# Two first layers, second half of the tokens: block products of a 2x2 scheme in place of the plain matmuls

## The chip, the cores and the metric

One core of one Trainium2 chip runs the whole program. The metric is device time in microseconds (us); lower is better. The engines are TensorE (PE in the profile: matrix products, with PEld for its weight loads), VectorE (DVE), ScalarE (ACT), GpSimd (POOL), and SyncE (SP), which issues most DMAs. Each engine takes its instructions in the order in which the program gives them, and waits on semaphores for the others.

## The reference

```python
def _attn_ref(q, k, v, w_pre, w_post):
    scores = np.matmul(q, k.transpose(0, 1, 3, 2)) / np.sqrt(64)
    scores = np.einsum('bhij,hg->bgij', scores, w_pre)
    scores = scores - np.max(scores, axis=-1, keepdims=True)
    attn = np.exp(scores)
    attn = attn / (np.sum(attn, axis=-1, keepdims=True) + 1e-09)
    attn = np.einsum('bhij,hg->bgij', attn, w_post)
    return np.matmul(attn, v)
def _moe_ref(x, w1, w2, w3, w_out):        # 768 -> 1024 -> 1024 -> 768
    return ((x @ w1) * (x @ w2) @ w3) @ w_out
def _moe2_ref(x, w_in, w_out):             # 768 -> 2048 -> 768
    h = np.maximum(x @ w_in, 0.0)
    return h * h @ w_out
# x = attention output of 4 batches x 448 tokens = 1792 tokens x 768 features
```

The weights of the two mixtures arrive as 64-bit floats and are brought to 32 bits on the chip.

## The kernel before

Attention fills the first 470 us or so. The change leaves it alone. It leaves its output in DRAM as `xd`, four blocks of 448 tokens.

The two mixtures then run over the tokens in two halves of 896, each half as two blocks (t = 0, 1) of 448 columns. Features lie on the partitions. A *unit* is one output chunk of 128 features: `l1` (x times a chunk of w1 or w2), `ly` (the product of both times w3·w_out, which `p34` has multiplied together once), `l3` (w_in, then relu and square) and `l4` (the second w_out). All operands are split into a high part (rounded to the matmul's 32-bit type, `fp32r`) and a low part (the rest), and `mm3` makes three matmuls for each 128-deep chunk: high·high, high·low, low·high. A matmul has 448 columns. An `l1` or `l3` unit has 6 chunks, so 18 matmuls for each block; a `ly` or `l4` unit has 8 chunks, 24 matmuls.

Weights come in pieces of 384 or 512 columns. For each piece, in both halves alike, SP loads the 64-bit words (`raw`), ACT narrows them (L81), DVE joins the bits in three instructions (L93, L95, L97), ACT rounds to the high part (L111) and POOL subtracts for the low part (L115). `Moe.stage` issues these a fixed number of pieces ahead of the unit that PE runs, and `Moe.run` walks the units in order, so the program's order is one list of (unit, block) steps.

## Time and profile before

| | us |
|---|---|
| median of 3 runs | 1355.46 (1354.13 to 1357.52) |
| the profiled execution | 1355.44 |
| its span, first to last instruction | 1353.60 |

Columns of the views: "busy" is the time in which an engine ran instructions, "x" their number, "mean ns" the mean duration of one, "idle before" the time the engine stood still ahead of them and what ended it. Matmuls are pipelined, so their durations overlap. PEclk is the granted TensorE clock, 1.00 being the full 2.4 GHz.

### The profile page before, as it was taken

The numbers are of one execution on the slowest core, as the hardware profiler recorded it, in microseconds if no ns is written. First come the engines' busy times: TensorE is split into PE (matmuls) and PEld (weight loads), VectorE is DVE, ScalarE is ACT, GpSimd is POOL, SyncE is SP. The second block draws the span as 40 slices with busy tenths as digits, with TensorE's granted clock in tenths as the row PEclk, the third lists the DMA queues.
The fourth block names the chain that finished last, engine by engine and source line by source line (L and its number), as shares of the span: only waits on it lengthen the run. The fifth ranks groups of instructions, "written<-read, shape, count | busy, mean of one in ns | idle before, by whom it ended". The sixth has DMA issues, their size and how long they took to land.

```text
span 1353.6 us, 23970 instructions
## 1 busy us (share of the span) xinstructions
PE 1317.1 (97%) x8858; PEld 1144.1 (85%) x8858; DVE 921.8 (68%) x1580; ACT 706.3 (52%) x1525; POOL 385.4 (28%) x405
## 2 busy tenths in 40 slices
PE   6999999999998899999999999999999999999998
PEld 3677777777776788899999999999999999999998
DVE  4898788888787789864228944985555128945972
ACT  5888878878886455433224533543343224533530
POOL 4143153244212312101222322233222222322231
PEclk9999999999999899999999999999999999999999
DMA  6565475466445556664123432465433133433441
GB/s 190 168 190 170 136 213 182 129 186 193 133 129 161 146 157 168 194 172 121 56 82 105 133 113 82 119 200 165 126 115 94 55 86 101 133 118 82 121 152 55
DMA packets 97033, 183.76 MB, mean 136 GB/s; under 512 B 20693, under 2 KB 63701, under 8 KB 96469
## 3 DMA queue, kind: packets, MB, share of 16 engines
q1 hardware_dynamic: 89717, 178.73, 45.5%
q10 hardware_dynamic: 7200, 3.51, 0.9%
q8 instruction: 70, 1.15, 0.4%
q14 instruction: 46, 0.38, 0.1%
HBM read 129.52 MB, written 14.16 MB: 106 GB/s over the span
## 4 chain that ended last, share of the span: by engine, by line
PE 78%; issue 7%; ACT 5%; DVE 4%; POOL 3%; DMA 2%; SPq 0%; ACTq 0%; POOLq 0%; DVEq 0%
PE l L54 47%; PE y L54 9%; PE sp L285 6%; PE p L54 5%; PE tp L341 5%; PE pv L382 4%; PE sc L259 4%; ACT p L299 2%; DMA kraw<-k 1%; POOL wl L115 1%; ACT ph L324 1%; POOL ql L242 1%; ACT s L270 1%; DMA qraw<-q 1%; DVE nm L291 1%
## 5 line engine op out<-in xcount | busy, mean ns | idle before, releaser
L115 POOL TENSOR_TENSOR wl<-f,wh 128x384 fp32r<-128x384 f32 (+1 forms) x176 | 197.8, 1126 | 566.3 <-ACT wh L111 539.5
L93 DVE TENSOR_SCALAR f<-y 128x384 int32<-128x384 int32 (+1 forms) x208 | 148.6, 714 | 91.8 <-POOL wl L115 88.5
L285 PE MATMUL sp<-r,kpre 120*120 120x448 f32 x360 | 159.4, 565 | 6.6 <-ACT p L299 3.0
L111 ACT ACTIVATE wh<-f 128x384 fp32r<-128x384 f32 (+1 forms) x192 | 106.6, 555 | 104.3 <-DVE f L97 96.0
L299 ACT ACTIVATE p<-sp,nm 120x448 f32<-120x448 f32 x180 | 113.7, 640 | 70.2 <-DVE nm L291 69.6
L54 PE MATMUL l<-bhh,wh 128*128 128x448 f32 x384 | 139.4, 363 | 0.0
L54 PE MATMUL l<-bhh,wl 128*128 128x448 f32 x384 | 139.2, 362 | 0.0
L54 PE MATMUL l<-blh,wh 128*128 128x448 f32 x384 | 138.2, 360 | 0.0
L291 DVE TENSOR_REDUCE nm<-sp 120x1 f32<-120x448 f32 x180 | 108.0, 619 | 42.3 <-PE sp L285 36.2
L97 DVE SCALAR_TENSOR_TENSOR f<-raw,f 128x384 int32<-128x384 int32 (+1 forms) x208 | 130.1, 625 | 7.2
L95 DVE SCALAR_TENSOR_TENSOR f<-y,f 128x384 int32<-128x384 int32 (+1 forms) x208 | 129.0, 620 | 7.0
L341 PEld LDWEIGHTS <-ph 120*128 120x128 f16 (+1 forms) x1440 | 107.7, 99 | 28.3 <-issue 27.9
L331 DVE SCALAR_TENSOR_TENSOR pl<-p,sm,ph 120x448 f16<-120x448 f32 x180 | 124.1, 730 | 0.0
L341 PE MATMUL tp<-kwh,ph 120*128 120x120 f16 x720 | 121.2, 218 | 2.8 <-DVE p L356 2.0
L341 PE MATMUL tp<-kwh,pl 120*128 120x120 f16 x720 | 120.3, 217 | 0.3 <-DVE pl L331 0.3
L341 PE MATMUL tp<-kwl,ph 120*128 120x120 f16 x720 | 120.4, 217 | 0.0
L81 ACT ACTIVATE y<-raw 128x384 f32<-128x384 f32 (+1 forms) x208 | 120.0, 577 | 0.2 <-DMA raw<-w3t 0.2
L324 ACT ACTIVATE ph<-p,sm 120x448 f16<-120x448 f32 x180 | 112.0, 683 | 15.3 <-DVE sm L319 15.1
L259 PE MATMUL sc<-kt,qh 128*110 128x448 f32 (+1 forms) x192 | 100.9, 525 | 9.5 <-DVE kt L220 7.3
L314 POOL TENSOR_SCALAR sm<-sm 120x2 f32<-120x2 f32 (+3 forms) x94 | 30.8, 328 | 276.1 <-ACT p L299 264.5
L285 PEld LDWEIGHTS sp<-r,kpre 120*120 120x120 f32 x360 | 59.2, 185 | 48.7 <-issue 21.9
L270 ACT ACTIVATE s<-sc 110x448 f32<-110x448 f32 (+1 forms) x186 | 90.6, 555 | 9.9 <-PE sc L259 8.0
(115 smaller groups left out, 3114.0 us busy)
## 6 DMA issues: line engine op xcount, KB each, us to landing
r<-s SPq DMA_DIRECT2D x172, 210.0 KB
raw<-w SPq DMA_DIRECT2D x64, 384.0 KB
raw<-win SPq DMA_DIRECT2D x64, 384.0 KB
raw<-wo SPq DMA_DIRECT2D x48, 512.0 KB
kraw<-k SPq DMA_DIRECT2D x22, 448.0 KB
raw<-w3t SPq DMA_DIRECT2D x16, 512.0 KB
qraw<-q SPq DMA_DIRECT2D x36, 220.0 KB
raw<-wo SPq DMA_DIRECT2D x16, 384.0 KB
```

Source lines behind the costliest of these rows:

```text
L54: nc.tensor.matmul(acc, w, x, start=(first and i == 0 and j == 0), stop=(last and i == n - 1 and j == 2))
L93: nc.vector.tensor_scalar(fi, yi, 3, 0x7FFFFFFF, ALU.logical_shift_left, ALU.bitwise_and)
L95: nc.vector.scalar_tensor_tensor(fi, yi, -0x80000000, fi, ALU.bitwise_and, ALU.bitwise_or)
L97: nc.vector.scalar_tensor_tensor(fi, raw[:, :, 0], 29, fi, ALU.logical_shift_right, ALU.bitwise_or)
L115: eng.tensor_tensor(self.out[i][1], self.ft.pop(i), f32(self.out[i][0]), ALU.subtract)
L259: nc.tensor.matmul(sc[:ic], t[:, hh * ic : hh * ic + ic], self.kt[b, h // 2][:, h % 2], start=(i == 0), stop=(i == 1))
L285: nc.tensor.matmul(t[:kk], self.kpre[:kk, :kk], self.rt.pop(g)[:kk], start=True, stop=True)
L291: nc.vector.tensor_reduce(nm[:kk], self.sp[g][:kk], AX.X, ALU.max, negate=True)
L299: nc.scalar.activation(p[:kk], self.sp.pop(g)[:kk], AF.Exp, bias=self.nm.pop(g)[:kk], accum_out=self.sm[g // 2][:kk, g % 2 : g % 2 + 1],)
L324: nc.scalar.activation(self.phl[g % NP][0][:kk, :S], self.pt[g][:kk], AF.Copy, scale=self.sm[g // 2][:kk, g % 2 : g % 2 + 1])
L331: nc.vector.scalar_tensor_tensor(l, self.pt.pop(g)[:kk], self.sm[g // 2][:kk, g % 2 : g % 2 + 1], h, ALU.mult, ALU.subtract)
L341: nc.tensor.matmul(t[:, j, :, :cnt], p[:kk, j * JP : j * JP + 128], w[:kk, :, :cnt], start=(i == 0), stop=(i == 2))
```

## The change

For the second half of the tokens, `l1` and `l3` no longer run as plain units. Their matrix product is cut into 2x2 blocks: the depth 768 in two halves of 3 chunks, the 896 tokens in their two blocks, and two output chunks side by side (for `l1`, the same chunk of w1 and of w2; for `l3`, two neighbouring chunks of w_in). Such a pair of chunks is called a *quad* in the code. Seven products of 9 matmuls (P1 to P7) replace eight, with sums and differences of weight blocks (S1 to S4) and of token blocks (T1 to T4) as operands, and extra additions to put the four results together (C11, C12, C21, C22). P6, P7 and P4 add into the PSUM bank that P1 began, and P3 into that of P5; ACT copies what stands in the bank in between.

During the first half, each joined 32-bit weight piece of w1, w2, w_in and the second w_out is also written to DRAM (`keep`), and the second half loads it from there, with no narrowing and no joining. The ring of joined pieces `f` grows from 2 to 4 buffers. The program's order is now made from a list of events with planned times (`event`, in us, kept in a heap); the first half's steps have the same order as before. Tiles and pads are laid out anew.

```diff
+    wf = {
+        "w1": dram.tile([8, 128, DM], F, name="w1f"),
...
     class Moe:
         def __init__(self, wp):
-            self.w = Weights(wp, PW, 4, 2, 2, 8, 8)
+            self.w = Weights(wp, PW, 4, 2, 4, 8, 8)
...
+        def keep(self, i):
+            if i in self.w.ft and self.pieces[i].get("keep") is not None:
+                nc.sync.dma_start(self.pieces[i]["keep"], self.w.ft[i])
...
+        def x_operands(self, start):
...
+            for c in range(3):
+                s = start + 15.0 * c
+                self.event(s - 24.0 - 12.0 * c, lambda c=c: load(c))
...
+        def stream(self, base, quads, ops, finish, first):
+            DUR, w, T = 1.8, self.w, {}
+            need = {
+                "P1": ("A11", "B11", "A"), "P2": ("A12", "B21", "B"), "P5": ("S1", "T1", "C"),
+                "P6": ("S2", "T2", "A"), "P7": ("S3", "T3", "A"), "P4": ("A22", "T4", "A"), "P3": ("S4", "B22", "C"),
+            }
...
+            def add(z, n, a, b, op):
...
+                nc.gpsimd.tensor_tensor(T[z, n], T[z, a], T[z, b], op)
+            def hi(z, pn):
...
+                cp(T[z, pn][0], T[z, need[pn][0]], AF.Copy)
+            def lo(z, pn, eng):
+                h, l = T[z, pn]
+                eng.tensor_tensor(l, T[z, need[pn][0]], f32(h), ALU.subtract)
...
+            def after(z, pn):
+                A, B_, C = (T.get((z, x)) for x in "ABC")
+                if pn in ("P1", "P6", "P7"):
+                    c = T[z, "c" + pn] = (first if pn == "P1" else self.tmp)(f"c{base}_{z}{pn}")
+                    cp(c, A, AF.Copy)
+                if pn == "P2":
+                    tt(T[z, "cP1"], B_, T[z, "cP1"], ALU.add)
+                    finish(z, "C11", T[z, "cP1"], None)
...
+            n = len(quads) // 2
+            for k in range(n):
+                slots = {
+                    "P1": 7 * k - 2 if k else 0, "P5": 7 * k + 1, "P6": 7 * k + 2, "P2": 7 * k + 3, "P7": 7 * k + 4,
+                    "P4": 7 * k + 6 if k < n - 1 else 7 * k + 5, "P3": 7 * k + 7 if k < n - 1 else 7 * k + 6,
+                }
+                for q in range(2):
+                    z, at = 2 * k + q, {pn: base + DUR * (2 * x + q) for pn, x in slots.items()}
+                    b = base + DUR * (14 * k + q)
+                    self.event(at["P1"] - 15.0, lambda z=z: load(z, 0))
+                    self.event(b - 8.2, lambda z=z: load(z, 1))
+                    for dt, a in (
+                        (-4.6, ("S1", "A21", "A22", ALU.add)), (-2.6, ("S2", "S1", "A11", ALU.subtract)),
+                        (2.4, ("S3", "A11", "A21", ALU.subtract)), (4.2, ("S4", "A12", "S2", ALU.subtract)),
+                    ):
+                        self.event(b + dt, lambda z=z, a=a: add(z, *a))
+                    for pn, t0 in at.items():
+                        eng = nc.vector if pn in ("P5", "P2", "P4") else nc.gpsimd
+                        self.event(t0 - 7.0, lambda z=z, pn=pn: hi(z, pn))
+                        self.event(t0 - 5.8, lambda z=z, pn=pn, eng=eng: lo(z, pn, eng))
+                        self.event(t0, lambda z=z, pn=pn: go(z, pn))
+                        self.event(t0 + DUR + 0.1, lambda z=z, pn=pn: after(z, pn))
+            return base + 14 * DUR * n
...
+        def square(self, f):
+            def finish(q, block, z, bank):
...
+                if bank is not None:
+                    nc.scalar.activation(z, bank, AF.Relu)
+                    self.split_chain(
+                        dst, ts, z, (0.9, lambda: nc.gpsimd.tensor_tensor(z, z, z, ALU.mult)), (0.4, lambda: None)
+                    )
+                else:
+                    self.split_chain(
+                        dst, ts, z, (0.7, lambda: nc.vector.scalar_tensor_tensor(z, z, 0.0, z, ALU.max, ALU.mult))
+                    )
...
+        def half1(self):
+            T = 0.0
+            ops = self.x_operands(-52.0)
+            T = self.stream(T, [(wf["w1"][m], wf["w2"][m]) for m in range(8)], ops, self.gate(), self.part)
...
+            for gr in range(2):
+                T = self.stream(
+                    T, [(wf["win"][8 * gr + f], wf["win"][8 * gr + f + 1]) for f in range(0, 8, 2)],
+                    lambda: D["y"], self.square(8 * gr), self.tmp,
+                )
```

`gate` (for `l1`) finishes with a multiply of both chunks, on POOL for one token block and on DVE for the other, `split_chain` makes the high part of a result on ACT and the low part on DVE.

How the instructions stand, at the two engines that feed PE in the `l3` layer of the second half. First POOL before the change: the low parts of the weight pieces (`wl`), one for each (unit, block) step of 3.6 us.

```order
L115 TENSOR_TENSOR wl176_12848<-f176_12843,wh176_12847 128x384
L115 TENSOR_TENSOR wl177_12887<-f177_12882,wh177_12886 128x384
L115 TENSOR_TENSOR wl178_12926<-f178_12921,wh178_12925 128x384
L115 TENSOR_TENSOR wl179_12965<-f179_12960,wh179_12964 128x384
L115 TENSOR_TENSOR wl180_13002<-f180_12997,wh180_13001 128x384
L115 TENSOR_TENSOR wl181_13039<-f181_13034,wh181_13038 128x384
```

POOL of the changed kernel, from the last low parts of the first pair of quads on. The long number is the stream's planned start; behind it stand the quad (0 to 3) and, for a low part, the product; a name that begins with 1_ to 4_ is a weight sum S1 to S4, and L983 is the square of a result.

```order
L884 TENSOR_TENSOR 158.40000000000006_0P3_13161<-4_158.40000000000006_0_13021,158.40000000000006_0P3_13160 128x384
L874 TENSOR_TENSOR 1_158.40000000000006_2_13187<-158.40000000000006_2_1_13140 128x384
L884 TENSOR_TENSOR 158.40000000000006_1P3_13185<-4_158.40000000000006_1_13041,158.40000000000006_1P3_13184 128x384
L874 TENSOR_TENSOR 1_158.40000000000006_3_13206<-158.40000000000006_3_1_13163 128x384
L874 TENSOR_TENSOR 2_158.40000000000006_2_13208<-1_158.40000000000006_2_13187,158.40000000000006_2_0_13003 128x384
L874 TENSOR_TENSOR 2_158.40000000000006_3_13224<-1_158.40000000000006_3_13206,158.40000000000006_3_0_13025 128x384
L983 TENSOR_TENSOR 158.40000000000006_0P7_13135<-158.40000000000006_0P7_13135 128x448
L983 TENSOR_TENSOR 158.40000000000006_1P7_13158<-158.40000000000006_1P7_13158 128x448
L884 TENSOR_TENSOR 158.40000000000006_2P6_13239<-2_158.40000000000006_2_13208,158.40000000000006_2P6_13238 128x384
L874 TENSOR_TENSOR 3_158.40000000000006_2_13259<-158.40000000000006_2_0_13003,158.40000000000006_2_1_13140 128x384
L884 TENSOR_TENSOR 158.40000000000006_3P6_13256<-2_158.40000000000006_3_13224,158.40000000000006_3P6_13255 128x384
```

Four low parts, the first two weight sums of the next pair and two squares now stand ahead of the low part of quad 2's P6.

DVE before, in the same layer: for each step the three joins (L93, L95, L97), a low part of a result (L628) and a square (L701).

```order
L93 TENSOR_SCALAR f184_13149<-y184_13108 128x384
L95 SCALAR_TENSOR_TENSOR f184_13149<-y184_13108,f184_13149 128x384
L97 SCALAR_TENSOR_TENSOR f184_13149<-raw184_13030,f184_13149 128x384
L628 TENSOR_TENSOR blh1_2_13120<-h21_2_0_13142,bhh1_2_13119 128x448
L701 TENSOR_TENSOR h21_2_1_13179<-r1_2_1_13177 128x448
```

DVE of the changed kernel, in the second pair of quads: L884 is a low part of a weight block, L949 one of a result, L918 an addition out of PSUM (bank C), L987 relu and square.

```order
L884 TENSOR_TENSOR 158.40000000000006_3P5_13222<-1_158.40000000000006_3_13206,158.40000000000006_3P5_13221 128x384
L949 TENSOR_TENSOR blh1_1_13145<-158.40000000000006_0P7_13135,bhh1_1_13144 128x448
L918 TENSOR_TENSOR 158.40000000000006_0P6_13066<-C158.40000000000006_0_13006,158.40000000000006_0P6_13066 128x448
L987 SCALAR_TENSOR_TENSOR 158.40000000000006_0P6_13066<-158.40000000000006_0P6_13066 128x448
L949 TENSOR_TENSOR blh1_3_13168<-158.40000000000006_1P7_13158,bhh1_3_13167 128x448
L918 TENSOR_TENSOR 158.40000000000006_1P6_13082<-C158.40000000000006_1_13028,158.40000000000006_1P6_13082 128x448
L949 TENSOR_TENSOR blh1_0_13100<-158.40000000000006_0P6_13066,bhh1_0_13099 128x448
L987 SCALAR_TENSOR_TENSOR 158.40000000000006_1P6_13082<-158.40000000000006_1P6_13082 128x448
L884 TENSOR_TENSOR 158.40000000000006_2P2_13277<-158.40000000000006_2_0_13003,158.40000000000006_2P2_13276 128x384
L949 TENSOR_TENSOR blh1_2_13118<-158.40000000000006_1P6_13082,bhh1_2_13117 128x448
L884 TENSOR_TENSOR 158.40000000000006_3P2_13300<-158.40000000000006_3_0_13025,158.40000000000006_3P2_13299 128x384
```

The joins are gone; the weight low parts of P2 (quads 2 and 3) now stand behind the finishing of the first pair's results.

Of the kernel before, what the change touches and what calls it, by code (L numbers as in the profile page):

```python
# [23 lines left out]
TB = 448  # L24
# [10 lines left out]
def fused_kernel(ctx, tc, q, k, v, w_pre, w_post, w1, w2, w3t, wo, win, wo2, eye, out):  # L35
# [9 lines left out]
    w34d = dram.tile([6, 128, 8, 128], F, name="w34d")  # L45

# [3 lines left out]
    def mm3(acc, terms, first=True, last=True):  # L50
        n = len(terms)
        for i, ((wh, wl), (xh, xl)) in enumerate(terms):
            for j, (w, x) in enumerate(((wh, xh), (wh, xl), (wl, xh))):
                nc.tensor.matmul(  # L54
                    acc, w, x, start=(first and i == 0 and j == 0), stop=(last and i == n - 1 and j == 2)
                )

    class Weights:
# [43 lines left out]
        def place(self, i, dst=None):  # L102
            n = self.ft[i].shape[1]
            if dst is None:
                hi = self.p.tile([128, self.wo], R, tag="wh", name=f"wh{i}", bufs=self.nhi)[:, :n]
# [366 lines left out]
    class Moe:  # L472
        def __init__(self, wp):
            self.w = Weights(wp, PW, 4, 2, 2, 8, 8)
            self.wp = wp
            self.xy, self.late, self.acc, self.ready = {}, [], {}, set()
            self.units, self.wot = [], {}
            for hf in range(2):
                l1 = [self.l1(hf, m, s) for m in range(8) for s in range(2)]
                if hf == 0:  # L480

                    wop = [self.wo_piece(c, h) for c in range(8) for h in range(2)]
                    mixed, rest = l1[:4] + wop[:6], wop[6:]
                    for i in range(8):
                        mixed.append(l1[4 + i])
                        for _ in range(1 + (i % 4 == 3)):
                            mixed.append(rest.pop(0))
                    assert not rest
                    l1 = mixed + [self.p34(m) for m in range(8)] + l1[12:]
                self.units += l1  # L490
                self.units += [self.ly(hf, n) for n in range(6)]
                for gr in range(2):
                    self.units += [self.l3(hf, 8 * gr + f) for f in range(8)]
                    self.units += [self.l4(hf, gr, e) for e in range(6)]
            self.pieces = [s for ss, _ in self.units for s in ss]
            n = np.cumsum([0] + [len(ss) for ss, _ in self.units])
            self.at = [int(x) for x in n]

        def stage(self, s, run=None):
            w = self.w  # L500
            ok = lambda i: 0 <= i < len(self.pieces)
            if ok(s + 6):
                w.load(s + 6, *self.pieces[s + 6][:2])
            if ok(s + 4):
                w.narrow(s + 4)
            if ok(s + 3):
                for part in range(3):
                    w.join(s + 3, part)
                to = self.pieces[s + 3][2:]
                w.place(s + 3, self.wot[to[0]] if to and to[0] else None)  # L510
            if ok(s + 2):
                w.rest(s + 2, nc.vector if self.pieces[s + 2][2:] else nc.gpsimd)
# [8 lines left out]
        def tail_plan(self):  # L521
# [6 lines left out]
            for i in range(11):  # L528
                t = TAIL["w"] + TAIL["ws"] * i if i < 8 else TAIL["w8"] + i
                at(t, lambda i=i: w.load(i, *self.pieces[i][:2]))  # L530
                if i < 9:
                    at(t + TAIL["n"], lambda i=i: w.narrow(i))
                if i < 8:
                    for part in range(3):
                        at(t + TAIL["n"] + 1 + part, lambda i=i, part=part: w.join(i, part))
                    at(t + TAIL["n"] + 4, lambda i=i: (w.place(i), w.high(i), w.rest(i)))
            for u in range(4):
                at(TAIL["x"] + TAIL["xs"] * u, lambda u=u: self.load_x(0, u))
                at(TAIL["x"] + TAIL["xn"] + TAIL["xt"] * u, lambda u=u: self.split_x(0, u))
            return ev  # L540

        def early(self, i, psum):

            ws = [self.w.out[2 * i + j] for j in range(2)]
            xh, xl = self.xy["x", 0, 0]
            assert all((0, u) in self.ready for u in range(4))
# [6 lines left out]
        def begin(self, ap_):  # L553
            self.ap = ap_

            for c in range(8):
                for e in range(2):
                    if c < 4:
                        t = ap_.tile([128, HT], R, tag=f"b{'hl'[e]}", name=f"wo{c}_{e}", bufs=10)
                        ts = t[:, :HC], t[:, TB : TB + HC]  # L560
                    elif c < 7:
                        ts = [ap_.tile([128, TB], R, tag="oa", name=f"wo{c}_{e}{h}", bufs=12)[:, :HC] for h in range(2)]
                    else:
                        ts = [ap_.tile([128, HC], R, tag="wx", name=f"wo{c}_{e}{h}", bufs=4) for h in range(2)]
                    for h in range(2):
                        self.wot[c, h] = (*self.wot.get((c, h), ()), ts[h])
            for u in range(4, 8):
                self.load_x(0, u)
# [3 lines left out]
        def run(self, ps):  # L572
            self.ps = ps
            order = [(2, 0), (3, 0), (0, 1), None, (1, 1), None, (2, 1), None, (3, 1)]
            for i in range(10, len(self.units)):
                order += [(i, t) if self.units[i][1] else None for t in range(len(self.units[i][0]))]
            for p, it in enumerate(order):
                if p == 1:
                    for u in range(4, 8):
                        self.split_x(0, u)  # L580

                def go():
                    i, t = it
                    ws = [self.w.out[self.at[i] + j] for j in range(2)]
                    self.units[i][1](ws, t, slice(t * TB, t * TB + TB))

                self.stage(p + 5, go if it else None)
# [3 lines left out]

        def new_xy(self, name, t):
            p = self.ap if t else self.wp
            out = []

            for e, before, after in (("h", 24, 0), ("l", 0, 48)):
                if t:
                    before = after = 0
                x = p.tile([128, before + 6 * TB + after], R, tag=f"xy{e}{t}", name=f"{name}{e}{t}")
                out.append(x[:, before : before + 6 * TB].rearrange("p (c n) -> p c n", n=TB))  # L600
            return tuple(out)

        def load_x(self, hf, u):
            t, u4 = divmod(u, 4)
            if u4 == 0:
                self.xy["x", hf, t] = self.new_xy(f"x{hf}", t)
            if u4 % 2 == 0:
                w = slice(CHUNKS[u4][0], sum(CHUNKS[u4 + 1][:2]))
                nc.sync.dma_start(f32(self.xy["x", hf, t][1][:, :, w]), xd[2 * hf + t, :, :, w])

        def split_x(self, hf, u):
            t, u4 = divmod(u, 4)
            o, ic, _ = CHUNKS[u4]
            xh, xl = (x[:, :, o : o + ic] for x in self.xy["x", hf, t])
            nc.scalar.activation(xh, f32(xl), AF.Copy)
            eng = nc.gpsimd if (u % 2 if hf else u < 4 or u == 5) else nc.vector
            eng.tensor_tensor(xl, f32(xl), f32(xh), ALU.subtract)
            self.ready.add((hf, u))

        def big(self, name):  # L620
            return tuple(
                self.ap.tile([128, HT], R, tag=f"b{e}", name=f"b{e}{name}", bufs=10) for e in "hl"
            )

        def split_late(self, dst, ts, p):
            def f():
                nc.scalar.activation(dst[0][:, ts], p, AF.Copy)
                nc.vector.tensor_tensor(dst[1][:, ts], p, f32(dst[0][:, ts]), ALU.subtract)  # L628

            self.late.append(f)  # L630
# [5 lines left out]
        def tmp(self, tag, name):  # L636
            return self.ap.tile([128, TB], F, tag=tag, name=name, bufs=2)

        def l1(self, hf, m, second):
            def run(ws, t, ts, acc=None):  # L640
                if second and t == 0:
                    self.xy["ab", hf, m] = self.big(f"ab{hf}_{m}")
# [201 lines left out]
```

## Rows read from the trace of the kernel before

**Rows 1.** Busy time by stretch in the second half: the l1 and the first l3 layer
```profile
core 0: us, PE busy (x) PEld busy (x) DVE busy (x) ACT busy (x) POOL busy (x), PEclk, DMA share, GB/s
946.60:1061.80 115.20, 115.20 (x577) 107.98 (x577) 58.89 (x118) 43.41 (x90) 33.16 (x32) 1.00 0.37 105
...
1119.40:1177.00 57.60, 57.60 (x289) 53.99 (x289) 52.99 (x77) 30.25 (x63) 17.30 (x16) 1.00 0.43 122
```
**Rows 2.** A group of TensorE's instructions, 946.6 to 1350 us
```profile
L54 PE MATMUL l<-x1h,wh 128*128 128x448 f32 x192 | 69.7, 363 | 0.0
```
**Rows 3.** Groups of DVE's instructions, 946.6 to 1349.8 us
```profile
L97 DVE SCALAR_TENSOR_TENSOR f<-raw,f 128x384 int32<-128x384 int32 x61 | 34.0, 558 | 2.1
...
L628 DVE TENSOR_TENSOR blh<-h,bhh 128x448 fp32r<-128x448 f32 x32 | 19.7, 617 | 0.0
...
L653 DVE TENSOR_TENSOR p<-l,a 128x448 f32<-128x448 f32 x16 | 10.0, 623 | 41.8 <-PE l L54 41.8
```
**Rows 4.** Groups of ACT's instructions, the same stretch
```profile
L111 ACT ACTIVATE wh<-f 128x384 fp32r<-128x384 f32 x61 | 31.6, 517 | 6.5 <-DVE f L97 6.5
L627 ACT ACTIVATE bhh<-h 128x448 fp32r<-128x448 f32 x32 | 18.4, 573 | 0.0
L699 ACT ACTIVATE r<-l 128x448 f32<-128x448 f32 x32 | 17.4, 545 | 54.6 <-PE l L54 54.6
```
**Rows 5.** POOL in order of time (start us, us) at five places
```profile
1012.65 2.00 POOL L115 TENSOR_TENSOR wl<-f,wh 128x384 fp32r<-128x384 f32 x2 [2.58 <-ACT wh L111]
...
906.83 1.30 POOL L115 TENSOR_TENSOR wl<-f,wh 128x512 fp32r<-128x512 f32 x1 [2.87 <-ACT wh L111]
908.08 1.63 POOL L617 TENSOR_TENSOR x1l<-x1l,x1h 128x660 fp32r<-128x660 f32 x1
...
771.86 1.43 POOL L115 TENSOR_TENSOR wl<-f,wh 128x512 fp32r<-128x512 f32 x1 [2.54 <-ACT wh L111]
...
81.24 2.24 POOL L220 TENSOR_TENSOR kt<-kraw,kt 64x448 fp32r<-64x448 f32 x2
...
320.85 2.62 POOL L220 TENSOR_TENSOR kt<-kraw,kt 64x448 fp32r<-64x448 f32 x2
```
**Rows 6.** DVE in order of time, beside or near some of them
```profile
904.16 0.42 DVE L93 TENSOR_SCALAR f<-y 128x512 int32<-128x512 int32 x1
...
908.42 0.62 DVE L725 TENSOR_TENSOR o<-l,oa 128x448 f32<-128x448 f32 x1 [1.64 <-PE l L54]
...
772.04 1.53 DVE L93 TENSOR_SCALAR f<-y 128x512 int32<-128x512 int32 x1
...
321.36 2.60 DVE L331 SCALAR_TENSOR_TENSOR pl<-p,sm,ph 120x448 f16<-120x448 f32 x2
```
**Rows 7.** TensorE in order of time at the start of p34
```profile
561.93 0.45 PE L54 MATMUL p<-wo,wl 128*128 128x384 f32 x1 [2.67 <-DVE wl L115]
...
562.87 0.84 PE L54 MATMUL p<-wo,wh 128*128 128x384 f32 x2
...
564.79 0.84 PE L54 MATMUL p<-wo,wh 128*128 128x384 f32 x2
...
565.75 0.62 PE L54 MATMUL p<-wo,wh 128*128 128x384 f32 x2
...
566.38 0.51 PE L54 MATMUL p<-wo,wh 128*128 128x384 f32 x2
...
567.42 0.51 PE L54 MATMUL p<-wo,wh 128*128 128x384 f32 x2
```
**Rows 8.** Busy time around it, columns as in rows 1
```profile
560.00:570.00 10.00, 8.07 (x37) 8.07 (x38) 9.53 (x16) 4.56 (x8) 0.00 (x0) 0.83 0.63 198
```
**Rows 9.** SP in order of time, as the first half begins
```profile
469.50 1.27 SPq L609 DMA_DIRECT2D x0l<-xd  x2
```
**Rows 10.** ACT in order of time, just after
```profile
477.00 2.72 ACT L615 ACTIVATE x0h<-x0l 128x660 fp32r<-128x660 f32 x4
```

More of the change, by code (lines that the diff above doesn't have):

```diff
@@ L54, in mm3 @@
                 nc.tensor.matmul(
-                    acc, w, x, start=(first and i == 0 and j == 0), stop=(last and i == n - 1 and j == 2)
+                    acc, w, x, start=(first and i == 0 and j == 0), stop=(last and i == n - 1 and j == 2), **kw
                 )
@@ L104, in place @@
             if dst is None:
+                if not self.out:
+                    self.p.tile([128, 48], F, tag="pad2", name="pad2")
                 hi = self.p.tile([128, self.wo], R, tag="wh", name=f"wh{i}", bufs=self.nhi)[:, :n]
@@ L576, in run @@
                 order += [(i, t) if self.units[i][1] else None for t in range(len(self.units[i][0]))]
+            self.events, self.clock = [], 0.0
+            t = -sum(self.units[it[0]][2] for it in order if it)
             for p, it in enumerate(order):
[L578 to L585, printed above, removed]
@@ L587, in run, with event, chain @@
-                self.stage(p + 5, go if it else None)
+                self.event(t, lambda p=p, it=it: self.step(p, it))
+                t += self.units[it[0]][2] if it else 0.0
+            self.half1()
+            while self.events:
+                self.clock, _, f = heapq.heappop(self.events)
+                f()
+        def event(self, t, f):
+            self.serial += 1
+            heapq.heappush(self.events, (round(t, 3), self.serial, f))
+        def chain(self, *steps):
+            t = self.clock
+            for dt, f in steps:
+                t += dt
+                self.event(t, f)
@@ L589, in psum, with step, go, six @@
+        def step(self, p, it):
+            if p == 1:
+                for u in range(4, 8):
+                    self.split_x(u)
+            def go():
+                i, t = it
+                ws = [self.w.out[self.at[i] + j] for j in range(2)]
+                self.units[i][1](ws, t, slice(t * TB, t * TB + TB))
+            self.stage(p + 5, go if it else None)
         def psum(self, name):
             return self.ps.tile([128, TB], F, tag="m", name=name, bufs=8)
+        def six(self, t, name):
+            p = self.ap if t else self.wp
+            x = p.tile([128, 6 * TB], R, tag=f"xy{t}", name=name, bufs=5 if t else 2)
+            return x.rearrange("p (c n) -> p c n", n=TB)
@@ L592, in new_xy @@
         def new_xy(self, name, t):
[L593 to L603, printed above, removed]
+            return tuple(self.six(t, f"{name}{e}{t}") for e in "hl")
@@ L630, in split_late @@
-            self.late.append(f)
+            self.late.append(lambda: self.split(dst, ts, p))
         def chunk(self, ws, c):
@@ new lines, in plain_weights @@
+        def plain_weights(self, tu, srcs):
+            w, keys = self.w, []
+            for i, src in enumerate(srcs):
+                k = ("p", round(tu, 3), i)
+                d = 2.4 * i
+                self.event(tu - 20 + d, lambda k=k, src=src: w.load(k, src, False))
+                self.event(tu - 12 + d, lambda k=k: (w.place(k), w.high(k)))
+                self.event(tu - 10 + d, lambda k=k: w.rest(k, nc.gpsimd))
+                keys.append(k)
+            return lambda: [w.out[k] for k in keys]
```

407 lines of the change are left out of this document (298 added, 109 removed).

## The prediction

> **What bounds the kernel now.** I read the stretches of the second half first. In the `l1` layer (115.2 us) and in the `l3` layer (57.6 us) TensorE is busy for the whole stretch at the full granted clock [rows 1], and none of its matmul groups there has any idle time ahead of it [rows 2]. So the second half goes as fast as TensorE issues matmuls: an `l3` layer is 16 steps of 18, 288 matmuls in 57.60 us, 0.200 us each (0.363 us is the duration of one, and they overlap). DVE, ACT and POOL are busy for 92%, 53% and 30% of that layer [rows 1]. They work ahead of TensorE and cost nothing as long as they stay ahead. Matmuls taken out come straight off the end; an engine that falls behind puts time back.
>
> **What comes off.** The matmuls concerned are six groups of 192 (x1h·wh, x1h·wl, x1l·wh, and the same with y1; one row stands for them) [rows 2], 1152 in all. Seven products for eight make it 1008: 144 fewer. All other matmuls stay. 144 x 0.200 = **28.8 us**. Every matmul keeps its 128x128 weights, its 448 columns and the place of its operands modulo 256 bytes (224 for the moving one, 160 for the weights, in both programs), so I keep the 0.200.
>
> **What the helpers get.** I write times from the start of a *stream* (one layer of block products) in planned us; a slot is 3.6 us (two products of 1.8, one of each quad), a pair of quads 7 slots, 25.2 us. A low part is planned 5.8 us ahead of its product, and the product needs it with its third matmul, 0.4 us after its start. Per pair in `l3`: ACT has 14 weight high parts of 0.517, 6 copies and 2 relus at 0.545, 8 result high parts of 0.573 [rows 4], 16.2 us of 25.2. POOL has 8 weight sums, 8 weight low parts and 2 squares. Two 384-column POOL operations in a row take 2.00 [rows 5], so 1.00 each; a 448-column one lies between that and the 1.30 of 512 columns [rows 5], 1.15. That is 18.3 us of 25.2. DVE has 6 weight low parts of 0.56, 14 operations on results with both inputs in SBUF (0.617) and 6 additions out of PSUM (0.623) [rows 3]: 15.7 us. Each fits alone.
>
> **But DVE and POOL hold each other up.** A DVE operation that took 0.42 us alone took 1.53 when it came 0.18 us into a POOL operation, and ended 0.28 after it; that POOL operation had begun under a DVE one and took 1.43 instead of 1.30. An addition with one input in PSUM beside a POOL operation kept its 0.62 [rows 5, 6]. Where both have work waiting they take turns: two POOL operations that take 2.24 took 2.62 with DVE operations waiting beside them, and the second began after one of these [rows 5, 6]. So one DVE operation let in costs POOL 0.38, and in a crowd DVE gets one such operation per turn of 1.00 + 0.38 = 1.38 us. Per `l3` pair that makes POOL 18.3 + 20 x 0.38 = 25.9 us for 25.2: full. In `l1`, where only 10 such DVE operations fall to a pair, 22.1.
>
> The Trainium skill ("SBUF — State Buffer", section "Who interferes with whom") says that a DVE instruction with two SBUF inputs and a GpSimd one that reads SBUF share a port pair, and that the later one fully blocks until the other ends. The rows agree that they exclude each other, but show an overlap at each change of hands. By the rule taken strictly the times of both simply add, as in the second rival below: 30.3 us for an `l3` pair and not 25.9, and a time of 1337 to 1349.
>
> **Where TensorE waits.** A stream of `l3` has only two pairs, and TensorE has the lead of 5.8 us, so the mean is not the trouble; the crowd in the middle is. At 19.4 POOL starts the list shown in the change: the square of quad 0 is the seventh and would be done at 19.4 + 6 x 1.00 + 1.15 + 5 x 0.38 (DVE operations planned there) = 28.4. The ACT copy behind it ends at 29.0, and the first L949 of DVE waits for it, planned at 26.6. All of DVE's list stands behind. The low part of P2 of quad 2 is the sixth two-input operation from there: 29.1 + 6 x 1.38 = 37.4, and TensorE needs it at 36.4: 1.0 late. That of quad 3 is two more turns on, 40.1, against 38.2 plus the 1.0 already lost: 0.9. POOL's own low part of P6 of quad 3, the eleventh, is out by about 33.7 for 34.6 and holds nobody. So 1.9 us per `l3` stream, **3.8** for two. In `l1` (four pairs) the low part of P2 of the second quad stands behind the finishing of quad 1, whose multiply is POOL's thirteenth: about 38.3 for 38.2. I put 0.3 on each of the three later pairs, **1.0**. Bounds: nothing, if POOL's list runs ahead of its plan, and the strict case below.
>
> Of the other edits, the copies out of a bank that is added to again have a slot or more (P6 two slots after P1, P4 at least one after P7) against 0.545; the joins that go were hidden under TensorE; the last additions after a stream (some 4 us) end before `l4` reaches their chunk (4.2 us into its first step). The weights need one load of the same 384 KB per two pieces instead of two, so DMA, at 0.37 to 0.43 in these layers [rows 1], is lighter; and the loads go out at least 8 us ahead of the product they feed. I cost these at nothing; should a copy or load be late, its own duration is the price, a few tenths to 3 us.
>
> **The first half.** It keeps its work and adds writes of 196 KB per piece. TensorE is the bound there too, but for its start: at 558.7 to 561.9 it waited 2.67 us for DVE, which is busy 9.53 of 10 us there [rows 7, 8]. SP now issues the last two of the first eight writes ahead of the x loads that stood at 469.50 [rows 9] and that ACT used from 477.00 [rows 10]. They go out once the last of these pieces is joined, three DVE instructions of some 0.56 [rows 3] or a little more later, 1 to 2 us; part of that is slack. What ACT loses there goes through DVE to p34. Against this, the `f` ring of four lets DVE start a join without waiting for POOL, worth little, since POOL shuts it out anyway. I take **+0.5** (bounds -1 and +3).
>
> **Sum.** Against the profiled execution (1355.44; the span is 1353.60, and the median of the runs, 1355.46, is the same): 1355.4 - 28.8 + 3.8 + 1.0 + 0.5 = 1331.9, so **1332 us**.
>
> **The rivals.**
> *Nothing waits.* If the pairs drift apart so that DVE's operations fall between POOL's, only the sum of matmuls counts: 1355.4 - 28.8 = 1326.6, with the start's bounds 1325.6 to 1329. For it: the low parts have 5 us in hand. Against it: the crowd at 19.4 to 38 has 14 POOL operations.
>
> *DVE and POOL strictly one after the other.* Then a turn is 1.00 + 0.617, an `l3` pair takes 18.3 + 6 x 0.56 + 14 x 0.617 = 30.3 us and overruns by 5.1, four pairs by 20.4. Of this the 5.8 us of lead can take one stream's share each, 11.6. So 8.8 to 20.4 come back instead of the 3.8: 1337 to 1349. Against it: the measured 0.38.
>
> *Slower than before.* Each of the eight pairs stops TensorE long enough for its clock to fall. The place is the chain POOL square, ACT copy, DVE list, TensorE above, with ACT's next high parts queued behind the copy as well. The price: after the 2.67 us wait the clock was granted at 0.83 over the 10 us [rows 8], and for 3.5 us (562.2 to 565.75) matmuls came at 0.32 us and not at the later 0.17 [rows 7], which is the 1.2 GHz level and costs 1.6 us more. Eight times 4.3 is 34.4, minus 28.8: 1361. It decides from 28.8 / 8 = 3.6 us per pair on. Against it: `l1` has 3 us of POOL free per pair, and the shorter waits that I expect are far from 2.67.
>
> *The writes slow the start.* If they hold up the x loads and the joins that bound 480 to 562, up to 5 us more: 1336.
>
> *The products do not save.* Set aside: the programs hold 144 fewer matmuls, and nothing changes in one.
>
> **Chances.** The forecast with waits of 2 to 8 us in all (1327 to 1335) 0.56; nothing waits 0.15; the slow start 0.06; strictly one after the other 0.15; slower 0.08. 1325 to 1343 leaves out the slower case and half of the strict one, 0.16. The likeliest case's own range is 1327 to 1335. About 0.3% (4 us) is what a measurement of this kernel can tell from no change, so: faster 0.89, same 0.03 (a strict case with stalls in `l1` too), slower 0.08.
>
> **What would show it.** The changed profile should have matmuls at 0.200 us and the second half's layers at 100.8 plus about 1 and 50.4 plus about 1.9 us; TensorE's waits should name DVE's low part of P2 in the second pair of each `l3` stream, at most 2 us each; DVE's two-input operations there should be stretched to 1 us and more by POOL, POOL's to about 1.4; the additions out of PSUM should stay at 0.62. The granted clock should stay at 1.00 after 570 us. The prediction is wrong if the waits name POOL, ACT copies or loads; if they are in every pair; or if the first half moves by more than 3 us.

## The result, and the profile after

The changed kernel takes 1342.57 us (median of 4 runs, 1341.39 to 1343.04), the kernel before 1356.49 in the runs beside it; the ratio is 0.9897, with a 95% interval of 0.988 to 0.9915. It is faster, by 13.9 us where the prediction had 23.5. The profiled execution has a span of 1340.8 us (1353.6 before), so the spans differ by 12.8.

Busy time by stretch in the changed kernel: the last `l4` layer of the first half, then the products of `l1`, and the two `l3` layers of products (columns as in rows 1, which these lines answer).
```profile
core 0: us, PE busy (x) PEld busy (x) DVE busy (x) ACT busy (x) POOL busy (x), PEclk, DMA share, GB/s
887.70:957.30 69.60, 61.41 (x289) 55.54 (x289) 53.97 (x64) 23.30 (x43) 33.38 (x24) 0.95 0.49 158
957.30:1058.10 100.80, 100.80 (x506) 94.48 (x505) 54.21 (x70) 46.56 (x96) 80.81 (x72) 1.00 0.21 66
1115.70:1168.90 53.20, 51.01 (x254) 47.05 (x253) 38.73 (x47) 29.06 (x60) 41.93 (x36) 1.00 0.19 60
1226.40:1279.30 52.90, 50.99 (x254) 47.13 (x253) 35.71 (x43) 27.47 (x57) 37.98 (x32) 1.00 0.20 60
```
The same `l4` layer in the kernel before:
```profile
889.00:946.60 57.60, 57.60 (x289) 53.99 (x289) 37.07 (x56) 20.85 (x36) 22.75 (x17) 1.00 0.62 190
```
The products do what was forecast: `l1` is 100.8 us for 115.2, with TensorE busy throughout, and the `l3` layers are 53.2 and 52.9 for 57.6. The `ly` and `l4` layers of the second half keep their 57.6. But a layer whose matmuls the change does not touch, the last of the first half, went from 57.6 to 69.6. By layer, from one span to the other:

| | us |
|---|---|
| 144 matmuls fewer | -28.8 |
| last `l4` layer of the first half | +12.0 |
| waits in the two `l3` layers | +2.8, +2.5 |
| waits in `l1` | 0.0 |
| everything up to that `l4` layer | -1.3 |
| sum | -12.8 |

TensorE's waits over the whole span, in us, times, longest:
```profile
PE l L61 <- POOL wl L124: 9.6, 8, 4.0
...
PE p L61 <- DVE wl L124: 2.8, 1, 2.8
...
PE 8.40000000000006_2_13148 L61 <- ACT .40000000000006_2P L905: 1.6, 1, 1.6
PE 66.4000000000002_2_14072 L61 <- ACT 6.4000000000002_2P L905: 1.6, 1, 1.6
...
PE 8.40000000000006_3_13352 L61 <- DVE .40000000000006_3P L884: 0.6, 1, 0.6
...
PE 66.4000000000002_3_14276 L61 <- DVE 6.4000000000002_3P L884: 0.3, 1, 0.3
```
The first line is new. 8.2 of its 9.6 us, five waits, lie in that `l4` layer; the longest, in order of time on four engines:
```profile
937.60 1.46 DVE L825 TENSOR_TENSOR x<-xs,x 128x448 f32<-128x448 f32 x1
938.99 1.52 DVE L100 TENSOR_SCALAR f<-y 128x512 int32<-128x512 int32 x1
940.54 0.69 DVE L102 SCALAR_TENSOR_TENSOR f<-y,f 128x512 int32<-128x512 int32 x1
941.27 0.69 DVE L104 SCALAR_TENSOR_TENSOR f<-raw,f 128x512 int32<-128x512 int32 x1
...
942.07 0.63 ACT L120 ACTIVATE wh<-f 128x512 fp32r<-128x512 f32 x1 [5.09 <-DVE f L104]
942.61 0.56 ACT L790 ACTIVATE xs<-xb 128x448 fp32r<-128x448 f32 x1
943.08 1.03 ACT L790 ACTIVATE xs<-x 128x448 fp32r<-128x448 f32 x2
...
943.73 1.13 POOL L791 TENSOR_TENSOR xs<-x,xs 128x448 fp32r<-128x448 f32 x1 [3.50 <-ACT xs L790]
944.81 1.51 POOL L791 TENSOR_TENSOR xs<-xs,xs 128x448 fp32r<-128x448 f32 x1
946.29 1.67 POOL L124 TENSOR_TENSOR wl<-f,wh 128x512 fp32r<-128x512 f32 x1
...
948.01 0.74 PE L61 MATMUL l<-bhh,wl 128*128 128x448 f32 x1 [4.05 <-POOL wl L124]
```
Read it from the end. TensorE waits for a low weight part (L124). POOL idled 3.50 us and then ran two low parts of the operands of x first (L791, lines of `x_operands`). They waited for ACT's copies (L790), which stood behind ACT's high weight part (L120), and that waited 5.09 us for DVE's join (L104), behind DVE's sums of x (L816 to L825). The low weight part's own input was there at 942.7; it began 3.6 us later. Three queues in order, each with operand work ahead of weight work. Behind that wait the granted clock fell:
```profile
946.00:956.00 10.00, 7.99 (x28) 7.26 (x29) 1.43 (x2) 1.05 (x2) 4.04 (x4) 0.66 0.44 153
```
In this stretch 12 matmuls came 0.37 us apart (the 1.2 GHz level) instead of 0.20. The layer's 12.0 us are 9.0 of waits, 2.5 of matmuls at the low clock and 0.5 of single slower ones behind a wait.

### The profile page after: what moved, and what is told of

Read it like the earlier page. It is cut to its first block, busy times and chain, and to the rows that moved or that the text cites. A ratio compares the mean times of both kernels' runs of the same rounds, so it can differ in the third digit from the quotient of the medians.

```text
span 1340.8 us, 23501 instructions
## 1 busy us (share of the span) xinstructions
PE 1290.5 (96%) x8714; PEld 1115.3 (83%) x8714; DVE 882.9 (66%) x1422; ACT 702.5 (52%) x1518; POOL 510.5 (38%) x505
## 5 line engine op out<-in xcount | busy, mean ns | idle before, releaser
L124 POOL TENSOR_TENSOR wl<-f,wh 128x384 fp32r<-128x384 f32 (+1 forms) x88 | 103.1, 1172 | 295.2 <-ACT wh L120 283.1
L100 DVE TENSOR_SCALAR f<-y 128x384 int32<-128x384 int32 (+1 forms) x120 | 94.9, 791 | 38.1 <-ACT y L88 38.1
L365 DVE TENSOR_SCALAR p<-tp,iv 112x480 f32<-112x480 f32 (+1 forms) x135 | 90.9, 701 | 2.6 <-PE tp L350 2.2
L120 ACT ACTIVATE wh<-f 128x384 fp32r<-128x384 f32 (+1 forms) x104 | 58.5, 562 | 64.6 <-DVE f L104 52.4
L391 PE MATMUL pv<-p,v 112*64 112x110 f32 (+1 forms) x1536 | 83.0, 266 | 1.8 <-DVE p L365 1.2
L104 DVE SCALAR_TENSOR_TENSOR f<-raw,f 128x384 int32<-128x384 int32 (+1 forms) x120 | 78.5, 654 | 4.1
L102 DVE SCALAR_TENSOR_TENSOR f<-y,f 128x384 int32<-128x384 int32 (+1 forms) x120 | 78.2, 652 | 4.0
L391 PEld LDWEIGHTS pv<-p,v 112*64 112x64 f32 x1536 | 76.0, 140 | 5.3 <-ACT y L88 1.4
L61 PE MATMUL l<-bhh,wl 128*128 128x448 f32 x192 | 71.3, 371 | 8.2 <-POOL wl L124 8.2
```

What stands on the lines that cost most here:

```text
L61: nc.tensor.matmul(acc, w, x, start=(first and i == 0 and j == 0), stop=(last and i == n - 1 and j == 2), **kw)
L100: nc.vector.tensor_scalar(fi, yi, 3, 0x7FFFFFFF, ALU.logical_shift_left, ALU.bitwise_and)
L124: eng.tensor_tensor(self.out[i][1], self.ft.pop(i), f32(self.out[i][0]), ALU.subtract)
L365: nc.vector.tensor_scalar(d, t, self.iv[:JP], None, ALU.mult)
L391: nc.tensor.matmul(t[64 * e : 64 * e + 64, x, :ic], self.v[b][:, j, g], self.p2[n][:, j, g, :ic], start=(j == 0), stop=(j == JC - 1),)
```

## The experiments

Theory 1: making the operands fills DVE. Theory 2: the writes of kept weights and loads of x delay the weight loads. Theory 3: in POOL's queue, low weight parts stand behind operand splits. The single executions below differ by up to 4 us in the attention ahead of all this (its end lies between 463 and 467 us), so I compare layers. Even a layer alone varies: the changed kernel and three of the runs below leave this `l4` layer as it is, and it took 69.6, 68.7, 68.65 and 69.5 us. A difference of 1 us in it says nothing.

**Without T1 to T4.**
```
-    self.event(s - 8.0, lambda c=c: load12(c))
-    for i in range(4):
-        self.event(s + 0.9 * i, lambda c=c, i=i: sums(c, i))
...
-    ("T1", nc.gpsimd), ("T3", nc.vector), ("T2", nc.gpsimd), ("T4", nc.vector),
     ("B11", nc.gpsimd), ("B21", nc.vector), ("B22", nc.gpsimd),
...
```


> Leaves out the operands T1 to T4 of the first mixture's products in the second half (12 sums, 12 of the 21 high/low splits, 3 loads); the products use B11 and B21 in their place. Looked at: the last l4 layer of the first half, 57.6 us before and 69.6 after the change. Theory 1 (making these operands fills DVE and the queues behind it, so low weight parts come late): 9 splits remain, 3 of them on DVE, so the layer takes 57.6 to 59.5 us and the kernel about 1331. Theory 2 (the writes of kept weights and the loads of x make weight loads late): all writes remain, so 66 to 70 us and about 1341. Theory 3 (only the order of POOL's queue, splits ahead of low weight parts): half of its splits remain, so about 63 us.


The layer took 57.6 us with no wait, and the kernel 1329.97:
```profile
887.20:944.80 57.60, 57.60 (x289) 53.99 (x289) 36.72 (x46) 17.08 (x31) 22.77 (x18) 1.00 0.55 179
```
All 12 us hang on the making of T1 to T4. Theory 2 had 66 or more, theory 3 in this simple form about 63; only theory 1 had the number.

**All low parts on POOL; all on DVE.**
```
-    ("T1", nc.gpsimd), ("T3", nc.vector), ("T2", nc.gpsimd), ("T4", nc.vector),
-    ("B11", nc.gpsimd), ("B21", nc.vector), ("B22", nc.gpsimd),
+    ("T1", E), ("T3", E), ("T2", E), ("T4", E), ("B11", E), ("B21", E), ("B22", E),   # E = nc.gpsimd, or nc.vector
```


> The 9 low parts that DVE makes of the first mixture's operands go to POOL (21 there, none on DVE). Theory 1 (DVE is full): DVE loses 9 operations of 0.62 to 1.7 us, so the last l4 layer of the first half takes 59 to 64 us instead of 69.6. Theory 3 (POOL's splits ahead of its low weight parts are what is late): three more of 1.15 us or more stand in each group, so 72 us or more. Theory 2 (DMA): 69 to 70, nothing changes.

> The 12 low parts that POOL makes of the first mixture's operands go to DVE (21 there, none on POOL). Theory 1 (DVE is full): 12 more operations of 0.62 us, 7.4 us, of which shorter DVE operations (less shared time with POOL, up to 0.4 us on each of 21) give some back: 68 to 76 us for the last l4 layer of the first half. Theory 3 (order of POOL's queue): low weight parts have POOL to themselves, so 58 to 61 us. Theory 2 (DMA): 69 to 70.


The layer in both, all on POOL and then all on DVE:
```profile
887.90:956.30 68.40, 61.89 (x290) 56.32 (x290) 49.20 (x55) 23.25 (x43) 44.23 (x33) 0.95 0.51 161
```
```profile
889.70:948.50 58.80, 58.10 (x290) 53.84 (x289) 50.96 (x76) 23.27 (x43) 14.93 (x11) 1.00 0.56 176
```
Theory 1 falls: 9 operations fewer on DVE gained 1.2 us, hardly more than the layer varies by itself, and 12 more gained 10.8. So DVE was not full. Theory 3 has the second run right (58.8) and the first wrong (72 forecast): 9 more splits on POOL did no harm there; that DVE's relief paid for them is likely, but not shown. All on DVE, the kernel took 1338.54: its attention ended 2.0 us later, and 4.8 us were lost in the `l1` products: TensorE waited 2.89 us there for POOL's low part of the second product, which stood behind a weight sum that waited 5.6 us for the first w2 load (issued on SP behind an `out` write), and the clock fell.

**The kept weights of this layer written twice.**
```
     nc.sync.dma_start(self.pieces[i]["keep"], self.w.ft[i])
+    if i >= len(self.pieces) - 12:
+        j = i - len(self.pieces) + 12
+        nc.sync.dma_start(twice[j], self.w.ft[i])
```


> The f32 weights of the last l4 layer of the first half are written to memory twice (12 more writes of 262 KB, to a place that nothing reads). At the 190 GB/s of that layer these are 16 us of all DMA engines. Theory 2 (DMA): the layer gets 5 us or more longer than 69.6. Theories 1 and 3: within 1 us of 69.6, kernel within 2 us of 1342.6.


DMA's share of the layer rose from 0.49 to 0.61 and the layer took 68.6 us (69.6), the `l1` products 101.8 (100.8). The layer's 1 us is within what it varies by, and 5 or more were forecast, so theory 2 falls. (The kernel's 1345.88 us are 3.3 more than 1342.6: its attention ended 2.1 us later and its p34 took 1.25 more.)

**Low weight parts on DVE, splits on POOL.**
```
-    return self.source("wo2", e, 1024 * gr, PW), run, 4.8
+    return [dict(z, dve=gr == 1) for z in self.source("wo2", e, 1024 * gr, PW)], run, 4.8
```
and all splits on POOL, as above.


> In the last l4 layer of the first half DVE makes the 12 low weight parts and POOL all 21 low parts of operands, so no low weight part stands behind a split on POOL, and POOL still has 21 operations that lengthen DVE's. If the lengthening alone makes DVE late: 64 us or more for the layer (DVE has 3 operations more than in the changed kernel). If the order of POOL's queue, where a low weight part waits behind splits that themselves wait for ACT and DVE, is what makes the time: 57.6 to 60.


60.2 us (60 at most was forecast for the order of the queue, 64 or more for the lengthening), kernel 1336.49. Compare it with the changed kernel: in this layer POOL runs 23 operations for 24, DVE 64 for 64, and DVE's three joins (L100, L102, L104) take 2.67 us a piece on the mean for 2.77. The load and the lengthening are nearly the same; what has gone is the low weight part behind splits in POOL's queue, and with it 9.4 of the 12 us. So the queue's order is the main part. The 2.6 us that remain are waits for DVE's low weight parts, behind sums and joins that POOL lengthens (L825 to 1.42 us on the mean; 0.61 in the run with all low parts on DVE). The longest of them:
```profile
920.04 1.40 DVE L825 TENSOR_TENSOR x<-xs,x 128x448 f32<-128x448 f32 x1
921.36 1.38 DVE L100 TENSOR_SCALAR f<-y 128x512 int32<-128x512 int32 x1
...
924.11 0.68 DVE L124 TENSOR_TENSOR wl<-f,wh 128x512 fp32r<-128x512 f32 x1
...
924.85 0.47 PE L61 MATMUL l<-bhh,wl 128*128 128x448 f32 x1 [1.41 <-DVE wl L124]
```

**Later.**
```
-    s = start + 15.0 * c
+    s = (-26.0, -15.0, -6.0)[c]
...
```


> The same sums and splits of the first mixture's operands on the same engines, but begun 26, 15 and 6 us ahead of the second half instead of 52, 37 and 22, with B11 first. The run with all low parts on DVE made the last l4 layer of the first half 58.6 us with 12 more operations on DVE, so DVE alone isn't full. Theory 1, mended (POOL and DVE lengthen each other, and POOL's low weight parts stand behind splits, while weights are still being made): only the first group and half of the second meet weights, so that layer takes 58 to 63 us; what is late at the start of the second half costs 0 to 3. Kernel 1332 to 1336. Rival (the extra work itself costs, wherever it stands): the 12 us come again in the first 20 us of the second half, kernel 1341 or more.


The layer took 57.9 us, the `l1` products 107.9, the kernel 1338.11. Both readings have a part: the 12 us went, and 7.1 came back at the start of the second half, with a first wait of 2.22 us for POOL's low part of the operands (L791). Behind that wait the clock fell too, and three waits for low weight parts came after it (1.18 and 0.26 us for POOL's, 0.54 for DVE's). In both places operand work collided with a stage that has low weight parts on POOL. The kernel's time met neither forecast (1332 to 1336, and 1341 or more).

**The copies of `l3`.** In the `l3` layers ACT's copy of P7 out of its bank (L905) came late, and P4 could not start. ACT and TensorE in the changed kernel, the first of these layers:
```profile
1160.54 0.58 ACT L948 ACTIVATE bhh<-.40000000000006_3P 128x448 fp32r<-128x448 f32 x1 [1.38 <-DVE .40000000000006_3P L987]
1161.02 0.53 ACT L905 ACTIVATE .40000000000006_2P<-8.40000000000006_2_13148 128x448 f32<-128x448 f32 x1
...
1161.60 1.68 PE L61 MATMUL 8.40000000000006_2_13148<-ys,.40000000000006_2P 128*128 128x448 f32 x7 [1.62 <-ACT .40000000000006_2P L905]
```
The bank was ready at about 1158.2; the copy waited for the high part of C11 of the other quad (L948), and that for DVE's square (L987). First with C22 and C12 moved too, then C11 alone:
```
     (0.7, lambda: nc.vector.scalar_tensor_tensor(z, z, 0.0, z, ALU.max, ALU.mult)),
+    *([(0.6, lambda: None)] if block == "C11" else []),
```


> In both l3 streams the ACT copy that makes the high part of C11 is issued 0.6 us later, behind the copy of P7 out of its bank. In the profile of the changed kernel TensorE waited 1.78 us in each of these layers for that copy, which stood behind the high part of C11 of the other quad, itself waiting for DVE. Theory (order of ACT's queue): that wait goes or falls to 0.5 at most, the layers take 51.3 and 51.0 us instead of 53.2 and 52.9, kernel 3 to 3.6 less, 1339. Rival (ACT is late as a whole, or DVE behind it): the wait moves to another copy or low part and under 1 us is won.

> As the run with the later high part, but for C11 alone: C22 and C12 keep their times (in the other run C22's high part was read after C21 had overwritten its tile, so part of that run's output was another one). Theory (order of ACT's queue): the l3 layers take 50.9 to 51.5 us instead of 53.2 and 52.9, and l4 behind them 57.6 again; kernel 3.5 to 4.5 less than 1342.6 if the first half is the same. If only the wrong tile made it quick: 53 us again.


With all three the layers took 50.9 and 50.6 us, but `l4` behind them 58.4 twice (57.6). With C11 alone they took 51.24 and 50.96, `l4` 57.7, the kernel 1337.69. The order of ACT's queue cost 1.9 us per layer, where the plan had the two 0.2 us apart; `l4` behind gave 0.1 of it back.

**The squares on DVE.**
```
-    (0.9, lambda: nc.gpsimd.tensor_tensor(z, z, z, ALU.mult))
+    (0.9, lambda: nc.vector.tensor_tensor(z, z, z, ALU.mult))
```


> The squares of C21 and C12 in the l3 streams go from POOL to DVE (8 in each stream). The prediction's chain (POOL square, ACT copy, then DVE's list) is taken away: DVE's list in the second pair starts about 2 us earlier and has 2 operations more in it; POOL's has 2 fewer. If the chain makes the low part of P2 late: the 0.74 and 0.45 us waits for it go, and the 1.78 us wait for the ACT copy, which comes from the same lateness, falls too; layers 50.4 to 52 us. If DVE's turns with POOL alone make it late: the wait stays at 0.5 to 1.5 us, layers 53 to 54.


54.6 and 54.4 us. Neither forecast of the time was met. The waits for P2's low part went (0.05 and nothing remain), so the chain through POOL's square made it late, as the prediction said. But the wait for the copy grew from 1.78 us to 2.48 and 2.31, since DVE's square of C11, ahead of it through ACT, came later with more work on DVE; and behind it the clock fell.

**Three edits together,** and with them P2 earlier.
```
+    if base == 0.0 and k == 0:
+        self.event(-20.0, lambda z=z: load(z, 0))
+        self.event(-15.0 + 5.0 * q, lambda z=z: load(z, 1))
...
+    d = 2.0 if n == 2 and k == 1 and pn == "P2" else 0.0     # the second run only
...
```


> Three edits on the changed kernel: all 21 low parts of the first mixture's operands on DVE, the first four weight loads of the second half at 20, 20, 15 and 10 us ahead instead of 15, 13.2, 8.2 and 6.4, and the C11 high part of l3 0.6 us later. Expected by the runs before: last l4 layer of the first half 58 to 59 us (69.6), l1 products 100.8 (105.6 with the low parts on DVE and the late loads: 2.9 us wait for POOL, which waited for the first w2 load, and 2 us of low clock), l3 50.9 to 51.5 twice. 1342.6 - 10.8 - 4 = 1328, 1325 to 1331, ratio 0.977 to 0.982 against the kernel before. If the wait at the start of the second half isn't the late load: 1332 to 1334.

> The three edits of the run before, and in the second pair of both l3 streams the high and low weight parts of P2 2 us earlier in the queues of ACT and DVE. If the late low part of P2 of quad 3 is a place in DVE's list, as the prediction has it: TensorE's gaps of 0.72 and 0.44 us there go, the layers take 50.5 and 50.5 us instead of 51.25 and 50.95, 1.2 us in all. If DVE is full there: what is put back (a square or a result's low part) makes the next bank's copy late, as with the squares on DVE, and 51.2 us or more remain.


The three edits give 1328.98 us (median of 5, 1327.08 to 1330.72), ratio 0.9802 against the kernel before (0.9781 to 0.9823): the layers are 58.8, 100.8, 51.25 and 50.95. This beats both kernels. With P2 earlier the gaps ahead of P2's low parts went, and `l3` fell to 51.05 and 50.63, between the two forecasts. But in the first layer the copy of P7 was late again (by 0.36 us), and `l4` behind both rose from 57.7 to 58.0: 217.7 us for the four layers, 217.6 without. On the sum the rival has it: what P2 gets is given back behind it.

## Why the prediction was right, and where not

The measured time lies inside the range of 1325 to 1343, 0.4 us below its upper end, and misses the likeliest case's 1327 to 1335. By the prediction's own signs the account was wrong: the waits name POOL and ACT copies, the first half moved by 10.7 us where 3 was the limit, and the clock did not stay at 1.00 after 570 us. It was right on what the change saves and wrong on where time would be lost; that the number fell into the range is partly luck.

*What comes off*: right. 144 matmuls at 0.200 us; `l1` is 14.4 us shorter, and the `l3` layers 7.2 each before waits.

*DVE and POOL take turns*: right where both have work waiting. In the second pair of `l3`:
```profile
1146.10 1.40 POOL L874 TENSOR_TENSOR 8.40000000000006_2_13259<-40000000000006_2_0_13003,40000000000006_2_1_13140 128x384 f32<-128x384 f32 x1
1147.46 1.40 POOL L884 TENSOR_TENSOR .40000000000006_3P<-8.40000000000006_3_13224,.40000000000006_3P 128x384 fp32r<-128x384 f32 x1
...
1144.52 0.73 DVE L949 TENSOR_TENSOR blh<-.40000000000006_0P,bhh 128x448 fp32r<-128x448 f32 x1 [2.41 <-ACT bhh L948]
1145.17 0.61 DVE L918 TENSOR_TENSOR .40000000000006_0P<-8.40000000000006_0_13006,.40000000000006_0P 128x448 f32<-128x448 f32 x1
1145.82 0.80 DVE L987 SCALAR_TENSOR_TENSOR .40000000000006_0P<-.40000000000006_0P 128x448 f32<-128x448 f32 x1
1146.54 1.44 DVE L949 TENSOR_TENSOR blh<-.40000000000006_1P,bhh 128x448 fp32r<-128x448 f32 x1
1147.90 0.61 DVE L918 TENSOR_TENSOR .40000000000006_1P<-8.40000000000006_1_13028,.40000000000006_1P 128x448 f32<-128x448 f32 x1
1148.44 0.91 DVE L949 TENSOR_TENSOR blh<-.40000000000006_0P,bhh 128x448 fp32r<-128x448 f32 x1
1149.27 1.43 DVE L987 SCALAR_TENSOR_TENSOR .40000000000006_1P<-.40000000000006_1P 128x448 f32<-128x448 f32 x1
1150.62 1.38 DVE L884 TENSOR_TENSOR .40000000000006_2P<-40000000000006_2_0_13003,.40000000000006_2P 128x384 fp32r<-128x384 f32 x1
1151.92 1.44 DVE L949 TENSOR_TENSOR blh<-.40000000000006_1P,bhh 128x448 fp32r<-128x448 f32 x1
1153.28 1.38 DVE L884 TENSOR_TENSOR .40000000000006_3P<-40000000000006_3_0_13025,.40000000000006_3P 128x384 fp32r<-128x384 f32 x1
1154.58 1.38 DVE L884 TENSOR_TENSOR .40000000000006_2P<-40000000000006_2_1_13140,.40000000000006_2P 128x384 fp32r<-128x384 f32 x1
1155.88 0.61 DVE L907 TENSOR_TENSOR .40000000000006_2P<-8.40000000000006_2_13336,.40000000000006_2P 128x448 f32<-128x448 f32 x1
```
POOL's operations start 1.36 us apart, where the prediction had 1.38, and the additions with an input in PSUM (L918, L907) keep their 0.61. One after the other, an operation of 1.00 and one of 0.62 would be 1.62; the measured turn is 1.36, so the two overlap by some 0.26 at the changes of hands. The Trainium skill ("SBUF — State Buffer", section "Who interferes with whom") has the later of the two block until the other ends; the trace agrees but for this overlap.

*Waits in `l3`*: the place right, the size wrong, one releaser missed. The chain through POOL's square came as forecast: the first L949 began 28.8 us into the stream (29.1 forecast). But three of the six two-input operations from there took 0.73 to 0.91 us and not a full turn of 1.38, so P2's low part of quad 2 was there at 36.3 and not 37.4, in time (1.0 late was forecast). That of quad 3 was late by 0.84 and 0.55 us (0.9 forecast). So of the 3.8 us forecast 1.4 came. What filled the rest is a step that failed: that the copies out of a bank that is added to again "have a slot or more" against 0.545 and cost nothing. A slot is enough for the copy alone, but it stood in ACT's queue behind a part that waits for DVE, and that took 1.78 us per layer (the step between two matmuls less the usual 0.20; the view above counts 1.62 of it as idle). With single slower matmuls behind the waits the sum is 5.2 us; that it isn't further from 3.8 is luck.

*Waits in `l1`*: none, for the 1.0. POOL was busy 20.2 us of each pair's 25.2, where 22.1 was forecast.

*The first half's start*: no loss, for +0.5. The `l1` layer there is 0.7 us shorter, the attention ends 0.85 later, and 1.25 of the -1.3 is the clock (below). The writes cost nothing that shows, though DMA's share at 470 to 480 rose from 0.80 to 0.93.

*What the sum lacked*: the largest term. That the first half "keeps its work" is the step that failed most: the sum has no line for `x_operands`, whose 12 sums, 21 splits and their copies are issued 52 to 12 us ahead of the second half, in a layer that had DVE busy for 37 of 57.6 us and POOL for 23. Counted by busy time they fit there: 21 operations of 0.62 make 50 us on DVE, and 12 of 1.15 make 37 on POOL. In the order of three queues they do not. Without that, the forecast would have been met within 2 us: 1342.6 - 12.0 = 1330.6 for 1331.9. That nearness is luck too: the waits in `l3` were 1.4 more than forecast, those in `l1` 1.0 less, and the start of the first half 1.8 less, 1.25 of it by the clock. The rivals on the start's writes, on DVE and POOL strictly in turn, and on a stop in every pair did not come. The time lies in the strict rival's 1337 to 1349 as well, but the turns are 1.36 us and not the 1.62 that it needs.

How much POOL and DVE lengthening each other adds is known in part. With the low weight parts out of POOL's queue and the lengthening nearly as before, 2.6 us remained. How much of the other 9.4 the order would have cost without the lengthening stays open: no run took away one operation's lengthening and kept the order.

## What to carry to other kernels

Work that prepares a later stage belongs in the sum of the stage in which it is issued, and it is not enough that it fits there by busy time: ask of each queue what stands behind it, and who waits for that. Keep preparation that waits for another engine out of the queue that makes the last operands of the matmuls now running; here it was cheaper on the busier engine. Where two steps stand 0.2 us apart in a plan and the first waits for another engine, put the one that TensorE waits for first.

## What the runs showed of the hardware that was not expected

The clock does not always fall behind the same wait. At the start of p34 TensorE stops for 3.1 us from one matmul to the next in the changed kernel and all 11 variants of it (3.0 before). In 7 of these 12, and before [rows 8], the clock then falls and the p34 stage takes 71.15 us; in 5, the changed kernel among them, it takes 69.90. In the changed kernel the stretch stays at full clock:
```profile
560.00:570.00 10.00, 8.08 (x45) 7.76 (x46) 9.73 (x18) 4.55 (x8) 0.00 (x0) 1.00 0.60 194
```
Nor does the longer wait always cost more: in the `l4` layer of the changed kernel one of 2.87 us (at 934) left the matmuls behind it at 0.20 us, and in the run with the operands later one of 2.22 us was followed by matmuls 0.37 apart. At p34, 1.25 us of a kernel's time hang on this, so a difference of that size between single executions says nothing unless the layers are compared.
